# Weights of a two-layer MoE kernel converted in pairs of slots: one change to an attention and MoE kernel on Trainium2

## The chip, the core and the metric

The kernel runs on one core of one Trainium2 chip. The metric is the device time of one execution in microseconds (us). Of the engines of the core, PE does the matrix products (PEld is its weight load), DVE the vector arithmetic, ACT the activations and copies, POOL a few elementwise products, and SP issues all DMA transfers in one queue.

## The reference, cut to what matters

```python
B, H, S, D = 4, 8, 576, 64
# causal attention, mixed with a linear memory
a = softmax(causal(q @ k.T / sqrt(D)));  local = a @ v
q_p = elu(q) + 1
mem_out = (q_p @ M_prev) / (q_p @ z_prev + 1e-6)
x = sigmoid(beta) * mem_out + (1 - sigmoid(beta)) * local       # [2304, 512]
# first MLP, d_ff 1536
x = (sigmoid(x @ w_gate) * (x @ w_val)) @ w_out
# second MLP, d_ff 2048
h = x @ w_in
out = (h * clip(h + 3, 0, 6) / 6) @ w_out2
```

Everything is 32-bit. The host passes the bits of each weight array as 64-bit integers (`wm1`, `wm2`), that is, as float64 values; the kernel makes from each value a pair of 32-bit parts, a rounded high part and the rest, and every product of the MLPs is made of three matmuls (`mm3`: high by high, high by low, low by high).

## The kernel before, in words

A weight **slot** is a block of 128 by 512 weights. There are 36 slots of the first MLP (for each of the 12 blocks f of its inner width: gate, value and output) and 32 of the second. A slot takes a DMA of 512 KB into a staging tile `wst` (`w_load`, L112 to L120) and nine operations over 512 columns (`w_convert`, L122 to L144): ACT takes the absolute value of the upper words into a scratch tile `wf` (L132); DVE clamps it, masks and shifts it, joins it with the sign bits (L133 to L135: the value now stands in `wf`) and writes its power of two over the upper words (L137); ACT writes the high part of the slot from `wf` (L140); DVE scales the lower words (L141), adds them to `wf` (L142) and writes the rest to the slot (L143). The upper and lower words of a value lie side by side in `wst`, so an operation on one of them reads or writes every second word.

The kernel has three phases. **Phase A** runs attention over 80 steps (32 visits of a pair of heads and a range of tokens, three or two blocks of queries each), and between its pieces the first half of the first MLP (f 0 to 5, 18 slots) over six chunks of 312 tokens. The order of PE's instructions is written out by hand (`FILL` says how many pieces of the MLP go into a step); the order on the other engines and on SP's queue is drawn up beforehand by a list scheduler that takes what is ready, earlier program text first, and stays fixed at run time. The 18 slots are converted in steps 6 to 31, one slot in two steps of three, with two staging tiles and two scratch tiles. A chunk's input comes from attention through HBM (`xd`): `pv` drains it to `xd`, row k of `xd` being pair k of heads, and `moe_x` loads a chunk with one DMA of 624 KB into `xc` and splits it in four quarters into `xs` (ACT the high part, DVE the rest).

**Phase B** does the other half of the first MLP (f 6 to 11) over five chunks; the first of them has all 12 blocks, as its tokens were not in phase A. Its 18 new slots, and then the 32 of the second MLP, are converted as the chunks go on, with three staging and three scratch tiles (the pool `wstage2`). Its staging opens when the attention buffers are given up. **Phase C** does the second MLP over six chunks of 384 tokens.

Of the kernel before, what the change touches and what calls it, by code (L numbers as in the profile page):

```python
# [10 lines left out]
I32 = mybir.dt.int32  # L11
# [29 lines left out]
    [_T[0][0:4], _T[0][4:8], _T[0][8:12]],  # L41
    [_T[1][4 * n : 4 * n + 4] for n in range(5)],
]
NW_A = 3 * NFA
NW_B = 3 * (FF1 - NFA)
NSTAGE = 3

FILL = (4, 9, 6, 9, 6, 6)

# [14 lines left out]
class Kernel:  # L64
# [41 lines left out]
        nc.vector.tensor_scalar_add(self.a2, self.a2, 1.0)  # L106


    def plan_weights(self, keys, pools):
        self.wkeys, self.wpools, self.wstaged = list(keys), list(pools), []  # L110

    def w_load(self):  # L112
        if not self.wkeys or len(self.wstaged) >= NSTAGE:
            return
        nc = self.nc
        key = self.wkeys.pop(0)
        src = self.wm1[key[1], key[2]] if key[0] == 1 else self.wm2[key[1], key[2]]
        st = self.stage.tile([128, 512, 2], I32, name="wst", tag="wst")
        nc.sync.dma_start(st.rearrange("p a b -> p (a b)"), src.bitcast(I32))
        self.wstaged.append((key, st, self.wpools.pop(0)))  # L120

    def w_convert(self):  # L122
        if not self.wstaged:
            return
        nc = self.nc
        key, st, pool = self.wstaged.pop(0)
        lo, hi = st[:, :, 0], st[:, :, 1]


        w = self.stage.tile([128, 512], F32, name="wf", tag="wf")  # L130
        wi = w.bitcast(I32)
        nc.scalar.activation(w, hi.bitcast(F32), AF.Abs)  # L132
        nc.vector.tensor_scalar(w, w, HI_MIN, HI_MAX, op0=ALU.max, op1=ALU.min)  # L133
        nc.vector.tensor_scalar(wi, wi, 0x07FFFFFF, 3, op0=ALU.bitwise_and, op1=ALU.logical_shift_left)
        nc.vector.scalar_tensor_tensor(wi, hi, -0x40000000, wi, op0=ALU.bitwise_and, op1=ALU.bitwise_or)  # L135

        nc.vector.tensor_scalar(hi, wi, -0x800000, None, op0=ALU.bitwise_and)  # L137
        sl = pool.tile([128, 2, 512], F32R, name="wslot", tag="wslot")
        lof, hif = lo.bitcast(F32), hi.bitcast(F32)
        nc.scalar.copy(sl[:, 0, :], w)  # L140
        nc.vector.scalar_tensor_tensor(lof, lo.bitcast(U32), 2.0**-52, hif, op0=ALU.mult, op1=ALU.mult)  # L141
        nc.vector.tensor_tensor(w, w, lof, op=ALU.add)  # L142
        nc.vector.tensor_tensor(sl[:, 1, :], w, sl[:, 0, :].bitcast(F32), op=ALU.subtract)  # L143
        self.w[key] = sl  # L144

    def weight(self, *key):
        while key not in self.w:
# [24 lines left out]
    def load_visit(self, v):  # L172
        if v >= len(VISITS):
            return
        nc = self.nc
        p, ranges = VISITS[v]
        b, h = PAIRS[p]
        qk = self.pa2.tile([128, 2, S], F32, name="qk", tag="qk")
        a = self.pa2.tile([128, 20 * D], F32, name="aux", tag="aux", bufs=3)
        qn = a[:, 0 : 10 * D].rearrange("p (e j d) -> p e j d", e=2, j=5)  # L180
        (t0, n), j0, j1 = RTOK[ranges[0]], RANGES[ranges[0]][0], RANGES[ranges[0]][-1] + 1
        src = self.aux[b, h // 2]
        nc.sync.dma_start(qk[:, 0, t0 : t0 + n], self.qk[b, h // 2, :, 0, t0 : t0 + n])
        nc.sync.dma_start(qk[:, 1, : t0 + n], self.qk[b, h // 2, :, 1, : t0 + n])
        if h == 0 and 0 in ranges:
            z = self.pa2.tile([128, H, D], F32, name="zz", tag="zz")
            nc.sync.dma_start(z, self.zz[b : b + 1].rearrange("o h d -> o (h d)").broadcast_to([128, H * D]))
            self.z = z
        nc.sync.dma_start(
            qn[:, :, j0:j1, :],  # L190
            src[:, 0 : 10 * D].rearrange("p (e j d) -> p e j d", e=2, j=5)[:, :, j0:j1, :],
        )
        v1 = 10 * D + j1 * 2 * D
        nc.sync.dma_start(a[:, 10 * D : v1], src[:, 10 * D : v1])
        self.visits[v] = {
            "pair": PAIRS[p],
            "ranges": ranges,
            "z": self.z,
            "qk": qk,
            "qn": qn,  # L200
            "v": a[:, 10 * D :].rearrange("p (j c) -> p j c", j=5),
        }
# [27 lines left out]
    def score_part(self, v, i, a, e):  # L230
# [6 lines left out]
        if n == 0 and a == 0:  # L237
            P = self.pa2.tile([128, 2, 2 * PW[1]], F32, name="P", tag="P", bufs=3)
            vs["P", rg] = P[:, :, : nb * PW[rg]].rearrange("p g (n c) -> p g n c", n=nb)
            vs["l", rg] = self.pa2.tile([128, 2, nb], F32, name=f"l{rg}", tag=f"l{rg}")  # L240
            vs["m", rg] = self.pa2.tile([128, 2, nb], F32, name=f"m{rg}", tag=f"m{rg}")
# [115 lines left out]

    def moe_x(self, c):

        x = self.pm1.tile([128, KT, CA], F32, name="xc", tag="xc")  # L360
        self.nc.sync.dma_start(x, self.xd[:, :, c * CA : c * CA + CA].rearrange("k p t -> p k t"))
        xs = []
        for k in range(KT):
            t = self.pm1.tile([128, 2, CA], F32R, name=f"xs{k}", tag=f"xs{k}")
            self.split(t[:, 0], t[:, 1], x[:, k], self.nc.scalar, self.nc.vector)
            xs.append((t[:, 0], t[:, 1]))
        self.xnext = (c, xs, self.step)

# [38 lines left out]
    def phase_a(self):  # L407
        nc, tc = self.nc, self.tc
        moe_ctx, att_ctx = ExitStack(), ExitStack()
        self.stage = self.pool(att_ctx, "wstage", 2)  # L410
        self.open_moe_a(moe_ctx)
        self.open_attention(att_ctx)
        keys = [(1, f, w) for f in range(NFA) for w in range(2)] + [(1, f, 2) for f in range(NFA)]
        self.plan_weights(keys, [self.wpool] * NW_A)
        steps = [(v, rg, i) for v, (p, ranges) in enumerate(VISITS) for rg in ranges for i in RANGES[rg]]
        nt = len(steps)
# [37 lines left out]
        while t < nt or tq or vq:  # L454
# [43 lines left out]
        self.wpool2 = self.pool(ctx, "wslots2", NW_B - 4)  # L498
# [4 lines left out]
        self.wpools = [self.wpool2] * (NW_B - 4)  # L503
        for _ in range(NSTAGE):
            self.w_load()
        n = 0
        while c < NCA or stream is not None:
            self.step += 1
            moe(8)
            if n < NW_B - 4 - NSTAGE:  # L510
# [5 lines left out]
        self.wpool3 = self.pool(ctx, "wslots3", 4)  # L516
        self.wpools += [self.wpool3] * 4

        self.wpools += [self.wpool] * NW_A + [self.wpool2] * (NW_B - 4) + [self.wpool3] * 4
        self.ps_a = self.pool(ctx, "ps_a", 4, space=PSUM)  # L520

    def w_next(self):
# [19 lines left out]
    def phase_b(self):  # L542
# [49 lines left out]
        for i, item in enumerate(work):  # L592
# [10 lines left out]
    def phase_c(self):  # L603
# [40 lines left out]
        for item in work:  # L644
# [1 line left out]
            if prev:  # L646
                g4(*prev)
            prev = (gs, *item)
            for _ in range(2):
                self.w_next()  # L650
        g4(*prev)


# [58 lines left out]
```

## Time and profile before

| | |
|---|---|
| median of 3 runs | 1122.33 us (1121.84 to 1122.83) |
| the profiled execution | 1121.96 us, of which the span of its instructions is 1120.2 us |
| PE busy | 1074.1 us (96% of the span) |
| DVE busy | 616.9 us (55%) |
| ACT busy | 517.9 us (46%) |
| moved by DMA | 98.54 MB, 88 GB/s over the span |

Busy times are unions over the whole span, and the kernel has stretches with different limits; so each stretch has to be read by itself. An engine runs its instructions in order: one that waits holds up all behind it.

### The profile page before, as it was taken

How to read it: one execution, taken by the hardware profiler on the slowest of the kernel's cores; microseconds unless marked ns; L12 is line 12 of the kernel's file. 1: busy time of each engine (PE TensorE's matmuls, PEld its weight loads, DVE VectorE, ACT ScalarE, POOL GpSimd, SP SyncE). 2: the span in 40 equal slices, each digit the busy share in tenths (PEclk: the TensorE clock that was granted, in tenths of full speed). 3: DMA queues.
4: the chain of work that ended last, by engine and by line, in shares of the span. 5: the costliest groups of instructions: out<-in, count | busy, mean ns of one | idle time of the engine just before them, and what ended most of it. 6: DMA issues, size and time to landing. Idle time of an engine off the chain costs nothing.

```text
span 1120.2 us, 16105 instructions
## 1 busy us (share of the span) xinstructions
PE 1074.1 (96%) x5984; PEld 925.4 (83%) x5984; DVE 616.9 (55%) x1589; ACT 517.9 (46%) x1179; POOL 55.8 (5%) x72
## 2 busy tenths in 40 slices
PE   6679789999999999999999999999999999999998
PEld 4347567887888789999888888989999998999997
DVE  7989945455545535999997338933223232322322
ACT  5788767456745664444443123423323232332322
POOL 2102101110111000000000000000000000000000
PEclk9989889999999999999999999999999999999999
DMA  5455533233233314433653315400001010010000
GB/s 181 155 186 156 148 91 103 86 96 105 81 91 91 104 45 162 143 117 134 207 165 107 104 35 183 149 1 29 29 1 57 1 57 1 1 57 1 29 1 29
DMA packets 57935, 98.54 MB, mean 88 GB/s; under 512 B 5376, under 2 KB 42240, under 8 KB 57856
## 3 DMA queue, kind: packets, MB, share of 16 engines
q1 hardware_dynamic: 57856, 97.51, 27.4%
q8 instruction: 47, 0.77, 0.3%
q14 instruction: 32, 0.26, 0.1%
HBM read 79.50 MB, written 17.99 MB: 87 GB/s over the span
## 4 chain that ended last, share of the span: by engine, by line
PE 84%; DVE 6%; ACT 5%; DMA 4%; issue 1%; SPq 0%; POOL 0%; ACTq 0%; DVEq 0%
PE g L161 11%; PE g L159 11%; PE g L160 11%; PE acc L634 6%; PE acc L635 6%; PE acc L636 6%; PE m L159 5%; PE m L161 4%; PE m L160 4%; PE pv L338 4%; PE s L249 4%; PE t L312 3%; PE acc L159 3%; PE acc L161 3%; PE acc L160 3%; DMA wst<-in_wm 2%
## 5 line engine op out<-in xcount | busy, mean ns | idle before, releaser
L160 PE MATMUL g<-xs,wslot 128*128 128x384 f32 (+2 forms) x672 | 235.3, 351 | 0.0
L161 PE MATMUL g<-xs,wslot 128*128 128x384 f32 (+2 forms) x672 | 235.0, 351 | 0.0
L159 PE MATMUL g<-xs,wslot 128*128 128x384 f32 (+2 forms) x672 | 231.0, 351 | 0.0
L623 DVE SCALAR_TENSOR_TENSOR th<-th,g 128x384 f32<-128x384 f32 x96 | 53.1, 554 | 223.0 <-ACT th L622 222.8
L622 ACT ACTIVATE th<-g,three 128x384 f32<-128x384 f32 x96 | 55.7, 582 | 220.9 <-PE g L161 216.6
L160 PEld LDWEIGHTS g<-xs,wslot 128*128 128x128 f32 x672 | 126.1, 188 | 9.1
L159 PEld LDWEIGHTS g<-xs,wslot 128*128 128x128 f32 x672 | 126.0, 188 | 8.6
L161 PEld LDWEIGHTS g<-xs,wslot 128*128 128x128 f32 x672 | 126.1, 188 | 6.9
L634 PE MATMUL acc<-wslot,hs 128*128 128x512 f32 x288 | 113.7, 395 | 0.0
L635 PE MATMUL acc<-wslot,hs 128*128 128x512 f32 x288 | 113.5, 394 | 0.0
L270 ACT ACTIVATE P<-P,m 128x64 f32<-128x64 f32 (+4 forms) x160 | 89.3, 560 | 45.1 <-DVE m L253 42.8
L636 PE MATMUL acc<-wslot,hs 128*128 128x512 f32 x288 | 109.1, 393 | 0.0
L155 DVE TENSOR_TENSOR hs<-th,hs 128x384 fp32r<-128x384 f32 (+2 forms) x132 | 76.0, 576 | 51.6 <-ACT hs L154 51.0
L154 ACT CAST hs<-th 128x384 fp32r<-128x384 f32 (+2 forms) x132 | 69.7, 529 | 74.6 <-DVE th L623 49.5
L159 PE MATMUL m<-xs,wslot 128*128 128x312 f32 x288 | 94.3, 327 | 0.0
L312 PEld LDWEIGHTS t<-ident,P 128*128 128x128 f32 x480 | 57.5, 148 | 38.5 <-issue 20.2
L312 PE MATMUL t<-ident,P 128*128 128x128 f32 x480 | 74.4, 293 | 14.7 <-issue 5.7
L160 PE MATMUL m<-xs,wslot 128*128 128x312 f32 x288 | 88.3, 306 | 0.0
L161 PE MATMUL m<-xs,wslot 128*128 128x312 f32 x288 | 87.9, 305 | 0.0
L249 PE MATMUL s<-qk 64*128 64x320 f32 (+4 forms) x384 | 78.6, 473 | 9.6 <-DMA qk<-in_qk 6.6
L253 DVE CUSTOM_DVE_ANT_0 P<-s,mask 128x320 f32<-128x320 f32 (+3 forms) x160 | 66.1, 428 | 29.0 <-PE s L249 28.7
L132 ACT ACTIVATE wf<-wst 128x512 f32<-128x512 f32 x68 | 46.0, 677 | 77.0 <-DMA wst<-in_wm 61.5
(74 smaller groups left out, 1793.6 us busy)
## 6 DMA issues: line engine op xcount, KB each, us to landing
wst<-in_wm SPq DMA_DIRECT2D x68, 512.0 KB, 3.6
aux<-in_aux SPq DMA_DIRECT2D x32, 192.0 KB, 2.5
qk<-in_qk SPq DMA_DIRECT2D x32, 160.0 KB, 3.2
aux<-in_aux SPq DMA_DIRECT2D x16, 320.0 KB, 3.5
qk<-in_qk SPq DMA_DIRECT2D x16, 288.0 KB, 3.1
x<-x SPq DMA_DIRECT2D x6, 768.0 KB, 4.4
out<-xp SPq DMA_DIRECT2D x18, 256.0 KB, 2.0
xc<-xd SPq DMA_DIRECT2D x6, 624.0 KB, 5.0
```

Source lines behind the costliest of these rows:

```text
L154: (ehi.copy if ehi is self.nc.scalar else ehi.tensor_copy)(hi, src)
L155: elo.tensor_tensor(lo, src, hi.bitcast(F32), op=ALU.subtract)
L159: nc.tensor.matmul(out, w[0], x[0], start=first, stop=False)
L160: nc.tensor.matmul(out, w[0], x[1], start=False, stop=False)
L161: nc.tensor.matmul(out, w[1], x[0], start=False, stop=last)
L249: nc.tensor.matmul(ps[:, : e - a], qk[rows, 0, q0 : q0 + 128], qk[rows, 1, a:e], start=True, stop=True)
L253: nc.vector.tensor_tensor_reduce(out=P[:, g, n, 64 + a : 64 + e], in0=ps[:, : e - a], in1=self.mask[:, off + a : off + e], scale=-0.125, s ...
L270: self.nc.scalar.activation(x, x, AF.Exp, bias=vs["m", rg][:, g, n : n + 1], scale=-1.0, accum_out=vs["l", rg][:, g, n : n + 1],)
L312: nc.tensor.transpose(ps[:, c : c + 128], src, self.ident)
L634: nc.tensor.matmul(a, gs[:, 0, cc], w[:, 0, :], start=(f == 0), stop=False)
L635: nc.tensor.matmul(a, gs[:, 0, cc], w[:, 1, :], start=False, stop=False)
L636: nc.tensor.matmul(a, gs[:, 1, cc], w[:, 0, :], start=False, stop=(f == FF2 - 1))
```

## The change

Weights are planned, loaded, staged and released two slots at a time. In phase A one conversion covers both slots, so each of the nine operations runs over 1024 columns (`wide` 2), with one scratch tile for conversions (before: two); the value is joined in place in the staging tile and the power of two stands in the scratch tile. In phases B and C a pair is loaded together and converted one slot after the other over 512 columns (`wide` 1), with two staging tiles of two slots (before: three of one) and one scratch tile (before: three). Phase A converts a pair in every third step. A chunk's input is loaded in four DMAs of a quarter each, into two buffers. The tile for `z_prev` has one buffer instead of two, and the tiles `l` and `m` share their buffers between the two ranges.

```diff
-NW_A = 3 * NFA
-NW_B = 3 * (FF1 - NFA)
-NSTAGE = 3
+NW_A = 3 * NFA // 2
+NW_B = 3 * (FF1 - NFA) // 2
+NLATE = 2
...
     def w_load(self):
-        if not self.wkeys or len(self.wstaged) >= NSTAGE:
+        if not self.wkeys or len(self.wstaged) >= 2:
             return
...
-        st = self.stage.tile([128, 512, 2], I32, name="wst", tag="wst")
-        nc.sync.dma_start(st.rearrange("p a b -> p (a b)"), src.bitcast(I32))
+        keys = self.wkeys.pop(0)
+        n = len(keys)
+        st = self.stage.tile([128, n, 512, 2], I32, name="wst", tag="wst")
+        for i, key in enumerate(keys):
+            src = self.wm1[key[1], key[2]] if key[0] == 1 else self.wm2[key[1], key[2]]
+            nc.sync.dma_start(st[:, i].rearrange("p a b -> p (a b)"), src.bitcast(I32))
...
+    def convert(self, sl, st):
+        nc = self.nc
+        lo, hi = st[:, :, :, 0], st[:, :, :, 1]
+        w = self.stage.tile([128, self.wide, 512], F32, name="wf", tag="wf", bufs=1)
+        wi, hif, lof = w.bitcast(I32), hi.bitcast(F32), lo.bitcast(F32)
+        nc.scalar.activation(w, hif, AF.Abs)
+        nc.vector.tensor_scalar(w, w, HI_MIN, HI_MAX, op0=ALU.max, op1=ALU.min)
+        nc.vector.tensor_scalar(wi, wi, 0x07FFFFFF, 3, op0=ALU.bitwise_and, op1=ALU.logical_shift_left)
+        nc.vector.scalar_tensor_tensor(hi, hi, -0x40000000, wi, op0=ALU.bitwise_and, op1=ALU.bitwise_or)
+        nc.vector.tensor_scalar(wi, hi, -0x800000, None, op0=ALU.bitwise_and)
+        nc.scalar.copy(sl[:, 0], hif)
+        nc.vector.scalar_tensor_tensor(lof, lo.bitcast(U32), 2.0**-52, w, op0=ALU.mult, op1=ALU.mult)
+        nc.vector.tensor_tensor(hif, hif, lof, op=ALU.add)
+        nc.vector.tensor_tensor(sl[:, 1], hif, sl[:, 0].bitcast(F32), op=ALU.subtract)
 
     def w_convert(self):
...
+        keys, st, pool = self.wstaged.pop(0)
+        sl = pool.tile([128, 2, len(keys), 512], F32R, name="wslot", tag="wslot")
+        for i in range(0, len(keys), self.wide):
+            self.convert(sl[:, :, i : i + self.wide], st[:, i : i + self.wide])
+        for i, key in enumerate(keys):
+            self.w[key] = sl[:, :, i]
...
-            z = self.pa2.tile([128, H, D], F32, name="zz", tag="zz")
+            z = self.pa2.tile([128, H, D], F32, name="zz", tag="zz", bufs=1)
...
-        x = self.pm1.tile([128, KT, CA], F32, name="xc", tag="xc")
-        self.nc.sync.dma_start(x, self.xd[:, :, c * CA : c * CA + CA].rearrange("k p t -> p k t"))
         xs = []
         for k in range(KT):
+            x = self.pm2.tile([128, CA], F32, name="xc", tag="xc")
+            self.nc.sync.dma_start(x, self.xd[k, :, c * CA : c * CA + CA])
             t = self.pm1.tile([128, 2, CA], F32R, name=f"xs{k}", tag=f"xs{k}")
-            self.split(t[:, 0], t[:, 1], x[:, k], self.nc.scalar, self.nc.vector)
+            self.split(t[:, 0], t[:, 1], x, self.nc.scalar, self.nc.vector)
...
-        self.stage = self.pool(att_ctx, "wstage", 2)
+        self.stage, self.wide = self.pool(att_ctx, "wstage", 2), 2
...
-        keys = [(1, f, w) for f in range(NFA) for w in range(2)] + [(1, f, 2) for f in range(NFA)]
+        keys = [[(1, f, w) for w in range(2)] for f in range(NFA)]
+        keys += [[(1, f, 2), (1, f + 1, 2)] for f in range(0, NFA, 2)]
...
-            if t >= 6 and t % 3 < 2:
+            if t >= 6 and t % 3 == 0:
                 self.w_convert()
...
-        self.stage = self.pool(ctx, "wstage2", NSTAGE)
+        self.stage, self.wide = self.pool(ctx, "wstage2", 2), 1
...
-        keys = [(1, f, w) for f in range(NFA, FF1) for w in range(3)]
-        keys += [(2, f, w) for f in range(FF2) for w in range(2)]
+        keys = []
+        for f in range(NFA, FF1, 2):
+            keys += [[(1, f, 0), (1, f, 1)], [(1, f + 1, 0), (1, f + 1, 1)], [(1, f, 2), (1, f + 1, 2)]]
+        keys += [[(2, f, 0), (2, f, 1)] for f in range(FF2)]
...
-            for _ in range(3 if i < 12 else 1 if i < 30 else 2):
+            for _ in range(2 - i % 2 if i < 12 else i % 2 if i < 30 else 1):
                 self.w_next()
```

## Rows read from the trace of the kernel before

**Rows 1.** Stretches: length, busy us (count) of PE PEld DVE ACT POOL; PEclk; DMA; GB/s

```profile
0.00:20.00 20.00, 11.81 (x42) 7.29 (x42) 12.07 (x54) 11.30 (x36) 4.31 (x11) 1.00 0.63 203
20.00:80.00 60.00, 41.87 (x226) 25.71 (x227) 53.56 (x168) 49.18 (x125) 9.28 (x11) 0.91 0.48 158
80.00:120.00 40.00, 38.23 (x278) 30.58 (x277) 38.96 (x116) 33.83 (x96) 9.68 (x9) 1.00 0.57 170
120.00:142.00 22.00, 13.94 (x67) 9.39 (x65) 21.11 (x57) 15.48 (x44) 2.94 (x4) 0.72 0.43 127
142.00:200.00 58.00, 54.09 (x344) 40.21 (x345) 26.19 (x102) 37.91 (x94) 5.87 (x8) 0.93 0.33 94
200.00:430.00 230.00, 228.82 (x1622) 190.67 (x1621) 112.28 (x421) 133.13 (x352) 23.77 (x30) 1.00 0.29 86
430.00:600.00 170.00, 169.57 (x863) 157.38 (x863) 158.21 (x316) 76.21 (x139) 0.00 (x0) 1.00 0.51 166
600.00:1110.00 510.00, 510.00 (x2528) 459.78 (x2527) 193.43 (x361) 158.21 (x293) 0.00 (x0) 1.00 0.13 41
```

**Rows 2.** What PE waited for, 0 to 150 us: total us, times, longest

```profile
PE m L161 <- DVE wslot L143: 6.8, 4, 3.6
PE t L312 <- issue: 5.7, 2, 5.4
PE m L159 <- ACT wslot L140: 1.1, 1, 1.1
```

**Rows 3.** DVE's groups over the span by shape: busy us, mean ns | idle before

```profile
L141 DVE SCALAR_TENSOR_TENSOR wst<-wst 128x512 f32<-128x512 uint32 x68 | 46.5, 684 | 0.1
L143 DVE TENSOR_TENSOR wslot<-wf,wslot 128x512 fp32r<-128x512 f32 x68 | 46.4, 682 | 0.0
L137 DVE TENSOR_SCALAR wst<-wf 128x512 int32<-128x512 int32 x68 | 30.2, 445 | 0.1
...
L133 DVE TENSOR_SCALAR wf<-wf 128x512 f32<-128x512 f32 x68 | 28.5, 420 | 13.3 <-ACT wf L132 12.9
...
L155 DVE TENSOR_TENSOR xs<-xc,xs 128x312 fp32r<-128x312 f32 x24 | 11.3, 495 | 14.6 <-ACT xs L154 14.6
```

**Rows 4.** DVE in order of time, two places: start us, us, instruction

```profile
100.12 0.67 DVE L143 TENSOR_TENSOR wslot<-wf,wslot 128x512 fp32r<-128x512 f32 x1
100.72 0.42 DVE L137 TENSOR_SCALAR wst<-wf 128x512 int32<-128x512 int32 x1
101.05 0.46 DVE L387 SCALAR_TENSOR_TENSOR th<-th,m 128x312 f32<-128x312 f32 x1
...
138.57 0.42 DVE L134 TENSOR_SCALAR wf<-wf 128x512 int32<-128x512 int32 x1
139.03 0.69 DVE L135 SCALAR_TENSOR_TENSOR wf<-wst,wf 128x512 int32<-128x512 int32 x1
...
141.01 0.69 DVE L142 TENSOR_TENSOR wf<-wf,wst 128x512 f32<-128x512 f32 x1
141.74 0.69 DVE L143 TENSOR_TENSOR wslot<-wf,wslot 128x512 fp32r<-128x512 f32 x1
```

**Rows 5.** ACT's two conversion groups over the span, by shape

```profile
L132 ACT ACTIVATE wf<-wst 128x512 f32<-128x512 f32 x68 | 46.0, 677 | 77.0 <-DMA wst<-in_wm 61.5 <-DVE wslot L143 5.0 <-DVE wf L142 3.3
...
L140 ACT CAST wslot<-wf 128x512 fp32r<-128x512 f32 x68 | 42.0, 617 | 33.3 <-DVE wf L135 27.0 <-PE g L161 6.0
```

**Rows 6.** What ACT waited for, 0 to 143 us

```profile
ACT wf L132 <- DMA wst<-in_wm: 8.8, 9, 2.0
```

**Rows 7.** ACT in order of time around the first chunk's input

```profile
65.57 1.51 ACT L154 CAST xs<-xc 128x312 fp32r<-128x312 f32 x4 [2.00 <-DMA xc<-xd]
```

**Rows 8.** Phase B: the first absolute value on ACT, in order of time

```profile
433.58 0.66 ACT L132 ACTIVATE wf<-wst 128x512 f32<-128x512 f32 x1 [0.63 <-DMA wst<-in_wm]
```

**Rows 9.** Phase B: slots finished by DVE from 430 to 510.7 us

```profile
L143 DVE TENSOR_TENSOR wslot<-wf,wslot 128x512 fp32r<-128x512 f32 x17 | 11.6, 683 | 0.0
```

**Rows 10.** Phase B: PE in order of time, output products of block f 10

```profile
525.34 0.75 PE L159 MATMUL acc<-hs,wslot 128*128 128x432 f32 x3
```

More of the change, by code (lines that the diff above doesn't have):

```diff
@@ L106, in attn_consts, with plan_weights @@
         nc.vector.tensor_scalar_add(self.a2, self.a2, 1.0)
-    def plan_weights(self, keys, pools):
-        self.wkeys, self.wpools, self.wstaged = list(keys), list(pools), []
+    def plan_weights(self, groups, pools):
+        self.wkeys, self.wpools, self.wstaged = list(groups), list(pools), []
     def w_load(self):
-        if not self.wkeys or len(self.wstaged) >= NSTAGE:
+        if not self.wkeys or len(self.wstaged) >= 2:
             return
         nc = self.nc
-        key = self.wkeys.pop(0)
-        src = self.wm1[key[1], key[2]] if key[0] == 1 else self.wm2[key[1], key[2]]
-        st = self.stage.tile([128, 512, 2], I32, name="wst", tag="wst")
-        nc.sync.dma_start(st.rearrange("p a b -> p (a b)"), src.bitcast(I32))
-        self.wstaged.append((key, st, self.wpools.pop(0)))
+        keys = self.wkeys.pop(0)
[4 more added lines that the diff above has]
+            nc.sync.dma_start(st[:, i].rearrange("p a b -> p (a b)"), src.bitcast(I32))
+        self.wstaged.append((keys, st, self.wpools.pop(0)))
+    def convert(self, sl, st):
[12 more added lines that the diff above has]
+        nc.vector.tensor_tensor(sl[:, 1], hif, sl[:, 0].bitcast(F32), op=ALU.subtract)
     def w_convert(self):
@@ L125, in w_convert @@
         nc = self.nc
[L126 to L144, printed above, removed]
+        keys, st, pool = self.wstaged.pop(0)
[4 more added lines that the diff above has]
+            self.w[key] = sl[:, :, i]
     def weight(self, *key):
@@ L239, in score_part @@
             vs["P", rg] = P[:, :, : nb * PW[rg]].rearrange("p g (n c) -> p g n c", n=nb)
-            vs["l", rg] = self.pa2.tile([128, 2, nb], F32, name=f"l{rg}", tag=f"l{rg}")
-            vs["m", rg] = self.pa2.tile([128, 2, nb], F32, name=f"m{rg}", tag=f"m{rg}")
+            vs["l", rg] = self.pa2.tile([128, 2, 3], F32, name="l", tag="l")[:, :, :nb]
+            vs["m", rg] = self.pa2.tile([128, 2, 3], F32, name="m", tag="m")[:, :, :nb]
         P, m, qk = vs["P", rg], vs["m", rg], vs["qk"]
@@ L495, in phase_a @@
         ctx = self.ctx
-        self.stage = self.pool(ctx, "wstage2", NSTAGE)
+        self.stage, self.wide = self.pool(ctx, "wstage2", 2), 1
         self.bx = self.pool(ctx, "bx", 1)
-        self.wpool2 = self.pool(ctx, "wslots2", NW_B - 4)
+        self.wpool2 = self.pool(ctx, "wslots2", NW_B - NLATE)
         self.ps_g = self.pool(ctx, "ps_g", 4, space=PSUM)
-        keys = [(1, f, w) for f in range(NFA, FF1) for w in range(3)]
-        keys += [(2, f, w) for f in range(FF2) for w in range(2)]
+        keys = []
+        for f in range(NFA, FF1, 2):
+            keys += [[(1, f, 0), (1, f, 1)], [(1, f + 1, 0), (1, f + 1, 1)], [(1, f, 2), (1, f + 1, 2)]]
+        keys += [[(2, f, 0), (2, f, 1)] for f in range(FF2)]
         self.plan_weights(keys, [])
-        self.wpools = [self.wpool2] * (NW_B - 4)
-        for _ in range(NSTAGE):
+        self.wpools = [self.wpool2] * (NW_B - NLATE)
+        for _ in range(2):
             self.w_load()
@@ L509, in phase_a @@
             moe(8)
-            if n < NW_B - 4 - NSTAGE:
+            if n < NW_B - NLATE - 2:
                 self.w_next()
@@ L515, in phase_a @@
         self.br = self.pool(ctx, "br", 1, side="right")
-        self.wpool3 = self.pool(ctx, "wslots3", 4)
-        self.wpools += [self.wpool3] * 4
-        self.wpools += [self.wpool] * NW_A + [self.wpool2] * (NW_B - 4) + [self.wpool3] * 4
+        self.wpool3 = self.pool(ctx, "wslots3", NLATE)
+        self.wpools += [self.wpool3] * NLATE
+        self.wpools += [self.wpool] * NW_A + [self.wpool2] * (NW_B - NLATE) + [self.wpool3] * NLATE
         self.ps_a = self.pool(ctx, "ps_a", 4, space=PSUM)
@@ L648, in phase_c @@
             prev = (gs, *item)
-            for _ in range(2):
-                self.w_next()
+            self.w_next()
         g4(*prev)
```

## The prediction

> **What bounds the kernel now.** I read the busy times by stretch first, since the page's averages mix stretches with different limits. From 200 us to 1110 us PE is busy for 908.4 of 910 us [rows 1]: the matmuls are the limit there, and DVE and ACT count only if they make PE wait. Before 200 us PE is idle 40 us: 8.2 us in the first 20 (first transfers), 18.1 from 20 to 80, 1.8 from 80 to 120, 8.1 from 120 to 142, and 3.9 after [rows 1]. From 20 to 142 us DVE is busy 113.6 of 122 us [rows 1]; it is the fullest engine there, with attention and the 18 conversions of phase A. So the change can be paid only out of the 28 us that PE idles between 20 and 142, or by making PE wait later.
>
> Then I asked what ended PE's waits in the first 150 us. Some 7.9 us end at the two operations that finish a slot, L143 and L140 [rows 2]: PE stands at output matmuls of the first chunk until its last weights are there. The last slot's L143 runs at 141.74 us [rows 4], just where the idle stretch ends. One wait of 5.4 us [rows 2] falls at 62 us, when ACT stands 2.0 us before the first chunk's input has landed [rows 7] and the rescaling of P, which PE's transposes want, is queued behind it. So the place where this change acts is the pace at which 18 slots get through DVE up to 142 us.
>
> **The change part by part.**
>
> *Fewer, longer operations in phase A.* Nine pairs replace 18 slots, so 9 x 7 = 63 DVE instructions vanish: 36 of the wide form (about 0.68 us for 512 columns) and 27 of the form that takes 0.42 us [rows 3]. Only the fixed part is saved. For the wide form, 512 columns take 0.682 us and 312 take 0.495 [rows 3], 0.94 ns a column, so 512 more columns cost 0.48 us; I take half of that, 0.24, for the fast form, which at 0.42 us cannot be going at that rate. How much of the fixed part is seen depends on the neighbour. With unrelated neighbours an operation follows a wide one after 0.60 us and a fast one after 0.33 us [rows 4]; fixed parts 0.12 and 0.09, so 36 x 0.12 + 27 x 0.09 = 6.8 us. Where each needs the one before, the starts are 0.73 and 0.46 us apart [rows 4]; fixed parts 0.25 and 0.22, or 14.9 us. The first is nearer: the stretch has two conversions and attention mixed. Against it: one scratch tile allows only one conversion in flight, so more of the operations left have their own predecessor as neighbour, at 0.13 us each (0.73 less 0.60), 63 x 0.13 = 8.2 us if all were mixed before and none after. I charge a third, 2.7. Net gain 4.0 us; bounds -1.4 to +14.9.
>
> *Strides.* The value now stands in every second word. L141 already reads and writes such words and takes 0.684 us against 0.682 for L143, with two dense operands [rows 3], so the wide form pays nothing. L137 writes them at 0.445 against 0.420 for L133 [rows 3]; reading them in the fast form isn't shown, and if it fell to the wide rate, nine masks would cost 9 x 2 x 0.26 = 4.7 us. I take 0, since the write does not fall. ACT's copy L140 becomes a strided read like L132: 0.677 against 0.617 [rows 5], 18 x 0.06 = 1.1 us more, against fixed parts of 18 ACT instructions saved. I take 0 for ACT; it has 23.5 us free from 20 to 142 [rows 1].
>
> *Deeper staging in phase A.* Two tiles of two slots hold twice as much ahead. ACT waits 8.8 us for staged weights in the first 143 us [rows 6], and DVE has 8.4 us of idle time from 20 to 142 [rows 1]. A wait ends later on both sides: the tile is now held to the last subtraction, and a pair's load is two DMAs. I take +2.0 us, a quarter; bounds 0 and 8.4. The price at the start: two more slots, 1 MB, go before the next visits' loads; at the 203 GB/s of the first stretch [rows 1] that is 5.2 us if all of it is in the way. The second `z_prev` buffer, 256 KB, may then no longer be loaded there, and DVE has converted slots to work on. I charge 1.0; bounds 0 and 5.2.
>
> *The input in quarters.* Row k of `xd` comes from one pair of heads, so three quarters needn't wait for the last pair. The third and fourth wait, in SP's queue, for ACT and DVE to free a buffer, and the loads of weights, queries and values behind them wait too. For the first chunk, ACT's 2.0 us [rows 7] and part of PE's 5.4 us [rows 2] can go; a late third quarter can cost the same again. I take +0.5; bounds -2 and +5.4. Later chunks have cover: PE idles 1.2 us from 200 to 430 us [rows 1].
>
> *Pairs as units.* The first slot of a pair is ready only when the second is. In the tail up to 142 us PE waits for the last one anyway, and from 80 to 120 us it is 96% busy [rows 1], so the first chunk's earlier weights had cover. I take 0.
>
> *Phases B and C.* Columns per operation stay, so DVE's work stays. What goes is the overlap: the next absolute value, on ACT, cannot start before the previous scaling L141 has read the one scratch tile. It has the addition and the subtraction behind it as cover, 2 x 0.73 = 1.46 us for 0.66 us [rows 4, 8]. Before, 17 slots took 77.1 us from the first absolute value at 433.58 us [rows 8, 9], 4.54 each; mixed, a slot's own operations take 4 x 0.60 + 3 x 0.33 = 3.39 [rows 4], which leaves 1.15 for the rest. One conversion at a time takes 4 x 0.73 + 3 x 0.46 = 4.30, so 4.30 to 5.45 with the rest. PE wants the 17th slot for block 10 at 525.34 us [rows 10]: allowed 91.8 / 17 = 5.40 each. I take 4.9 and no wait: 0, down to -1. Phase C's weights are converted where DVE has room: 38% busy from 600 us on [rows 1]. A fourth staged slot ahead of phase B's first input is 512 KB, 3 us at the 166 GB/s of that stretch [rows 1]; the tail of phase A's chunks on PE covers it.
>
> *Sum.* 4.0 + 2.0 - 1.0 + 0.5 = 5.5 us. The profiled execution took 1121.96 us (span 1120.2, 1.8 around it), 0.4 under the median of the three runs: 1116.5 us.
>
> **The rivals.** I call 0.2%, 2.2 us, about what a measurement here can tell from no change.
>
> *The whole fixed part comes back.* If the 63 instructions were worth their dependent spacing, 14.9 us, less the startup's 1.0 and with half of the staging wait, 4, the gain is 18; with only two thirds of it on PE's path, 12: 1110 us, reach 1106 to 1113. For it: the tail that PE waits on ends in dependent operations [rows 4], and ACT's waits for staging are real. Against it: PE's idle time from 80 to 120 us is only 1.8 us, so much of the gain there buys nothing. The Trainium skill ("VectorE: DVE Perf Modes", "The DRAIN you can't avoid") has a next operation start only when the pipe is empty, which would make the whole fixed part count; by its figure of 151 cycles at 0.96 GHz, 63 instructions are an estimated 9.9 us. This trace does not agree for mixed work: L137 starts at 100.72 us, 0.07 us before the L143 in front has ended [rows 4]. Chance 0.21.
>
> *The change gives its gain back.* One conversion in flight takes the whole 8.2 us, or the 1 MB at the start takes 5.2: 1120 to 1124 us, about 1122. For it: DVE has only 7% of idle time to lose [rows 1]. Chance 0.17.
>
> *Slower: phase B runs short of weights.* If ACT's absolute value is queued late (behind a tanh that waits for PE), its 0.66 us is not covered and a slot takes 5.45 + 0.66 = 6.1 us: the 17th is ready at 433.6 + 104 = 537.6, PE waits 12.3 us, less 5.5 gained, 1129 us. It decides from 433.6 + 17p > 525.3 + 5.5 + 2.2, p = 5.85 us a slot. For it: DVE is 93% busy there [rows 1]. Against: today's pace leaves 14.6 us in hand. Chance 0.14.
>
> **How the numbers follow.** The forecast, a gain of 2.2 to 8.5 us (1113.5 to 1119.8), has 0.48. Faster by over 0.2% are it and the first rival, 0.69; within 0.2% the second, 0.17; slower the third, 0.14. From 1108 to 1124.5 us lie the forecast, the second rival and some four fifths of the first, 0.82; the bounds of the unknown costs (startup -5.2, staging up to 8.4) end inside it.
>
> **What would show it.** Right: seven DVE groups of nine over 1024 columns in phase A at about 1.16 us (wide) and 0.66 us (fast); the last slot done some 5 us before 141.7 us and PE's waits on L143's successor cut by half; PE still 100% busy from 430 us. Wrong: a mask operation near 1.16 us (strided reads fall to the slow rate); PE idle in the first 20 us above 8.2 us by the startup's loads; PE waits on a scratch or slot tile between 490 and 540 us; SP held by the input's quarters before 200 us.

## The result, and the profile after

The changed kernel takes 1106.3 us (median of 4 runs, 1105.09 to 1108.91) against 1122.58 us for the kernel before in the same job: 16.3 us less. The ratio of the comparison is 0.987 [0.9853, 0.9888], which is 14.6 us (12.6 to 16.5); where kernels of different jobs are compared below, ratios are used. The forecast was 1116.5 us with a range of 1108 to 1124.5; the time lies below it. The direction was right, and the gain forecast, 5.5 us, was about a third of what came. One execution of a later kernel (the addition on POOL) took 1674.18 us at a granted clock of 0.577 and is left out below.

The profiled execution took 1105.09 us, of which the span is 1103.3 us, 16.9 us less than before. The head of the profile's page of the changed kernel:

```profile
span 1103.3 us, 16108 instructions
...
PE 1068.7 (97%) x5984; PEld 921.0 (83%) x5984; DVE 625.0 (57%) x1526; ACT 521.9 (47%) x1161; POOL 58.5 (5%) x72
```

Its stretches of busy time, with the columns of [rows 1]:

```profile
0.00:20.00 20.00, 12.64 (x50) 8.02 (x51) 12.79 (x52) 11.50 (x35) 5.72 (x12) 1.00 0.68 243
20.00:80.00 60.00, 43.90 (x241) 27.30 (x241) 59.23 (x157) 52.88 (x124) 12.42 (x12) 0.86 0.55 175
80.00:120.00 40.00, 39.10 (x287) 31.15 (x282) 38.51 (x95) 36.13 (x96) 7.46 (x9) 1.00 0.51 165
120.00:142.00 22.00, 19.64 (x121) 14.48 (x120) 20.27 (x57) 16.64 (x50) 3.71 (x5) 1.00 0.67 220
142.00:200.00 58.00, 56.18 (x393) 44.08 (x392) 33.85 (x124) 41.02 (x104) 7.35 (x9) 0.97 0.29 88
200.00:430.00 230.00, 228.48 (x1592) 190.53 (x1591) 118.44 (x416) 132.80 (x341) 21.89 (x28) 1.00 0.32 99
430.00:600.00 170.00, 170.00 (x844) 156.39 (x843) 151.47 (x281) 74.04 (x128) 0.00 (x0) 1.00 0.40 136
```

Against [rows 1] the 16.9 us divide in two. PE's idle time before 200 us falls from 40.1 to 28.5 us, 11.5 less: 0.8 in the first 20, 2.0 from 20 to 80, 0.9 from 80 to 120, 5.7 from 120 to 142, and 2.1 after. The other 5.4 us are busy time: the same 5984 matmuls keep PE busy 1068.7 us instead of 1074.1. The granted clock goes with it: 0.72 from 120 to 142 us before, 1.00 now; 0.93 and 0.97 from 142 to 200; against that 0.91 and 0.86 from 20 to 80. From 200 us on PE is all but full in both.

One number takes in both parts: the matmuls recorded before 200 us, the counts of the first five stretches. Before, 42 + 226 + 278 + 67 + 344 = 957; now 50 + 241 + 287 + 121 + 393 = 1092. At 228.48 / 1592 = 0.144 us for one in the stretch behind, 135 more by 200 us are 19.4 us of work that is not left for later. It overstates the 16.9 a little (the mix of shapes differs), but it goes with the time in all kernels below, and the table at the end of the experiments uses it. It is bookkeeping, not a cause: the matmuls are the same in number, so those not done by 200 us come later.

What PE and ACT waited for up to 143 us, and two of SP's waits, after two of SP's waits in the kernel before:

```profile
SPq L119 <- DVE wf L142: 28.8, 8, 10.4
SPq L361 <- DMA xd<-xpr: 2.3, 1, 2.3
```

```profile
PE m L171 <- DVE wslot L143: 1.9, 1, 1.9
...
ACT wf L134 <- DMA wst<-in_wm: 0.3, 1, 0.3
...
SPq L124 <- DVE wslot L143: 17.7, 4, 9.3
SPq L373 <- DMA xd<-xpr: 13.2, 7, 2.5
```

PE's waits on a slot fall from 7.9 us [rows 2] to 1.9, and ACT's waits for staged weights from 8.8 us [rows 6] to 0.3. The largest of SP's own waits for a staging tile was 28.8 us in eight waits in the kernel before; it is 17.7 in four. In exchange SP stands 13.2 us at the quarters of the input, which wait for attention's rows (2.3 us before).

DVE's groups of the pairs, by shape, and the one-slot form of the mask for comparison; then DVE in order of time at the last slot and at the first conversion of phase B:

```profile
L137 DVE SCALAR_TENSOR_TENSOR wst<-wst,wf 128x1024 int32<-128x1024 int32 x9 | 11.0, 1217 | 0.0
L143 DVE TENSOR_TENSOR wslot<-wst,wslot 128x1024 fp32r<-128x1024 f32 x9 | 10.9, 1216 | 0.1
...
L139 DVE TENSOR_SCALAR wf<-wst 128x1024 int32<-128x1024 int32 x9 | 7.6, 849 | 0.0
...
L139 DVE TENSOR_SCALAR wf<-wst 128x512 int32<-128x512 int32 x50 | 21.3, 425 | 1.1
...
126.96 1.22 DVE L143 TENSOR_TENSOR wslot<-wst,wslot 128x1024 fp32r<-128x1024 f32 x1
...
133.25 0.43 DVE L135 TENSOR_SCALAR wf<-wf 128x512 f32<-128x512 f32 x1 [0.73 <-ACT wf L134]
```

The last slot ends at 128.2 us instead of 142.4 [rows 4]: 14.2 us earlier, where the prediction said some 5. DVE's idle time from 20 to 80 us is gone (59.23 of 60 busy). The Trainium skill ("VectorE: DVE Perf Modes", the section on the TRN2 errata) puts the overhead of an operation on SBUF at a fixed amount per instruction; these rows agree: 1024 columns take 1.216 us, two operations of 512 take 2 x 0.682 [rows 3], so 0.15 us is saved for each operation taken away. "Vector Engine (DVE) Microarchitecture Reference" of the Trainium skill (section 5.2) gives 1.0417 ns a column; here (1216 - 682) / 512 is 1.043.

### The profile page after: what moved, and what is told of

It reads as the page before. It is cut to its first block, busy times and chain, and to the rows that moved or that the text cites. A ratio compares the mean times of both kernels' runs of the same rounds, so it can differ in the third digit from the quotient of the medians.

```text
span 1103.3 us, 16108 instructions
## 1 busy us (share of the span) xinstructions
PE 1068.7 (97%) x5984; PEld 921.0 (83%) x5984; DVE 625.0 (57%) x1526; ACT 521.9 (47%) x1161; POOL 58.5 (5%) x72
## 4 chain that ended last, share of the span: by engine, by line
PE 84%; DVE 6%; DMA 4%; ACT 3%; issue 1%; SPq 0%; POOL 0%; ACTq 0%; DVEq 0%
PE g L171 12%; PE g L170 12%; PE g L169 11%; PE acc L647 6%; PE acc L648 6%; PE acc L649 6%; PE m L169 5%; PE m L171 4%; PE m L170 4%; PE pv L348 4%; PE t L322 3%; PE s L259 3%; PE acc L171 3%; PE acc L169 3%; PE acc L170 3%; DMA xc<-xd 2%
## 5 line engine op out<-in xcount | busy, mean ns | idle before, releaser
L325 ACT COPY T<-t 128x512 f32<-128x512 f32 (+2 forms) x128 | 66.1, 541 | 9.8 <-PE t L322 9.7
```

The costliest lines, as they stand in the source:

```text
L325: nc.scalar.copy(pr["T", rg][:, o : o + c], ps[:, :c])
```

## The experiments

Each time below is a median beside the median of the kernel before in the same job; ratios carry their 95% interval. The changed kernel stands at 0.987.

**One slot at a time, still one scratch tile** (the changed kernel, phase A converting 512 columns per operation):

```diff
-        self.stage, self.wide = self.pool(att_ctx, "wstage", 2), 2
+        self.stage, self.wide = self.pool(att_ctx, "wstage", 2), 1
```

> The changed kernel, but in phase A a pair is converted slot by slot over 512 columns (one scratch tile); loads in pairs, staging and quarters stay. Theory columns (the gain comes from 63 fewer DVE operations): the last slot of phase A is done at 136 us or later instead of 128.3, PE waits on it for 4 us or more, and the time goes back to 1114 to 1120 us. Theory staging (the gain comes from loads that are ahead, ACT's 8.8 us of waits): the last slot stays before 131 us and the time at 1105 to 1110 us.

Measured: 1134.37 us against 1120.84, ratio 1.0115 [1.0094, 1.0135]. Both theories miss the time: it is some 27 us over the changed kernel and slower than the kernel before, though the marks of theory columns (a last slot after 136 us, PE waiting on slots for over 4 us) are there. A stretch of its busy times, and PE's largest waits on slots up to 200 us:

```profile
120.00:142.00 22.00, 9.21 (x25) 5.42 (x25) 20.75 (x47) 9.88 (x22) 0.70 (x1) 0.61 0.24 81
...
PE m L171 <- DVE wslot L143: 12.0, 7, 3.1
...
PE m L169 <- ACT wslot L140: 6.3, 5, 2.0
```

PE is busy 9 of 22 us there, and up to 200 us it stands 18.3 us at slots; the last one ends at 144.1 us. Two explanations remain: DVE's throughput with twice as many instructions, or the latency of one conversion after another through a single scratch tile.

**The same with two scratch tiles** separates them:

```diff
-        w = self.stage.tile([128, self.wide, 512], F32, name="wf", tag="wf", bufs=1)
+        w = self.stage.tile([128, self.wide, 512], F32, name="wf", tag="wf", bufs=self.nwf)
...
-        self.stage, self.wide = self.pool(att_ctx, "wstage", 2), 2
+        self.stage, self.wide = self.pool(att_ctx, "wstage", 2), 1
+        self.nwf = 2
...
+        self.nwf = 1
```

> The changed kernel with conversions over 512 columns in phase A, as in e1_narrow, but with two scratch tiles there, so that two conversions can be under way. Theory latency (what sets the pace of slots is the time from one absolute value to the scaling that frees the scratch tile; 1024 columns halve the number of such chains, two scratch tiles overlap them): the last slot moves back from 148 to 134 to 139 us and the time to 1110 to 1117 us, near e3_deep. Theory throughput (the sum of DVE's durations sets it, which e1_narrow and this kernel share): 1128 to 1137 us.

Measured: 1111.86 us against 1121.58, 0.9913 [0.9899, 0.9928]. So it was latency (the last slot ends at 131.3 us, earlier still than that theory had it; it was 144.1 with one tile, not 148): the second scratch tile is worth 1.0115 - 0.9913 of 1122 us, 22.7 us, at the same number of instructions. Seen from this kernel, the step to 1024 columns with one scratch tile is worth 0.9913 - 0.987, 4.8 us; from the kernel with one scratch tile it is worth 27.

**Quarters from the other side** (the kernel before, its input loaded in quarters, the tile for `z_prev` single, `l` and `m` shared between ranges; the staging and the conversions stay):

```diff
-        x = self.pm1.tile([128, KT, CA], F32, name="xc", tag="xc")
-        self.nc.sync.dma_start(x, self.xd[:, :, c * CA : c * CA + CA].rearrange("k p t -> p k t"))
...
+            x = self.pm2.tile([128, CA], F32, name="xc", tag="xc")
+            self.nc.sync.dma_start(x, self.xd[k, :, c * CA : c * CA + CA])
```

> The kernel before, with only the input in quarters, one buffer for z_prev and the shared l and m tiles. Theories columns and staging both: within 2 us of the kernel before (1120 to 1124 us). Theory quarters (ACT no longer stands before the first chunk's input, so the 5.4 us wait of PE goes): 1115 to 1119 us.

Measured: 1127.5 us against 1120.84, 1.0057 [1.0038, 1.0076]: 6.4 us slower, which no theory had. To see whether the tiles or the quarters do it, the quarters were put in alone:

> The kernel before with the four quarter loads of a chunk's input alone; the tiles for z_prev, l and m as before. Theory quarters cost (the third and fourth quarter wait in SP's queue and hold up loads behind them): 1125 to 1129 us, as e2_quarters. Theory tiles cost (one buffer for z_prev or the shared l and m tiles make e2_quarters slower): 1119 to 1122 us.

Measured: 1126.09 us against 1121.58, 1.0040 [1.0028, 1.0053]: 4.5 us slower by the quarters alone. Its waits of ACT and of SP up to 143 us, and its stretch from 160 to 200 us:

```profile
ACT wf L132 <- DMA wst<-in_wm: 9.8, 6, 3.3
...
SPq L363 <- DMA xd<-xpr: 15.6, 6, 4.0
...
160.00:200.00 40.00, 34.05 (x226) 25.62 (x227) 17.36 (x68) 27.59 (x67) 3.86 (x6) 0.96 0.33 98
```

SP, which issues everything in one queue, is held 15.6 us by quarters that wait for attention's rows to reach HBM; the kernel before shows 2.3 us of this. PE does 226 matmuls from 160 to 200 us; the kernel before does 251 there.

**Depth alone** (the kernel with quarters, and four staging tiles of one slot in phase A; 512 columns and two scratch tiles stay):

```diff
+        self.nst = 4
...
-        st = self.stage.tile([128, 512, 2], I32, name="wst", tag="wst")
+        st = self.stage.tile([128, 512, 2], I32, name="wst", tag="wst", bufs=self.nst)
...
-            if len(self.wstaged) < 2:
+            for _ in range(2):
                 self.w_load()
```

> The kernel before with the quarters and four staging tiles of one slot in phase A (as many slots ahead as in the changed kernel), conversions over 512 columns with two scratch tiles as before. Theory staging: ACT's waits for staged weights fall below 2 us, the last slot of phase A is done by 132 us, 1106 to 1113 us. Theory columns: DVE has the same work, the last slot stays after 136 us, 1116 to 1122 us.

Measured: 1113.72 us against 1120.84, 0.9932 [0.9912, 0.9952]. Against the kernel with quarters in the same job that is 13.8 us for depth (by the ratios 14.0, uncertain by some 3), in a kernel with the quarters; against the kernel before, depth, quarters and tiles together gain 7.1 us. Two of its stretches, and ACT's wait for staged weights up to 143 us:

```profile
20.00:80.00 60.00, 46.42 (x242) 28.83 (x242) 57.20 (x179) 51.97 (x132) 10.87 (x12) 0.86 0.54 171
...
142.00:200.00 58.00, 55.86 (x381) 43.11 (x378) 35.41 (x127) 41.41 (x101) 5.99 (x8) 0.97 0.40 114
...
ACT wf L132 <- DMA wst<-in_wm: 1.2, 1, 1.2
```

ACT's waits fall as theory staging had it, and the time is just past its range; its other mark, a last slot by 132 us, did not come. The last slot ends at 137.0 us, only 1.9 us before that of the kernel with quarters. Most of the gain lies behind it (the two profiled executions differ by 8.9 us): 381 matmuls from 142 to 200 us, where the kernel with quarters has 332 and the kernel before 344 [rows 1].

**Half the depth** (the changed kernel with one staging tile of two slots in phase A):

```diff
-        self.stage, self.wide = self.pool(att_ctx, "wstage", 2), 2
+        self.stage, self.wide = self.pool(att_ctx, "wstage", 1), 2
```

> The changed kernel with one staging tile of two slots in phase A instead of two, so that a pair is loaded only when the pair before is done. Theory staging (depth is worth about half of the gain or more): each of seven loads adds 4 to 5 us to the time between pairs, the last slot ends after 150 us, 1125 to 1150 us. Theory columns alone: below 1112 us.

Measured: 1154.05 us against 1121.58, 1.0285 [1.0268, 1.0302], some 47 us over the changed kernel and beyond even the range of theory staging. The last slot's subtraction starts at 169.44 us:

```profile
142.00:200.00 58.00, 33.60 (x170) 22.85 (x170) 26.06 (x65) 23.48 (x52) 2.68 (x4) 0.70 0.31 96
...
169.44 1.23 DVE L143 TENSOR_TENSOR wslot<-wst,wslot 128x1024 fp32r<-128x1024 f32 x1
```

DVE is busy less than half of this stretch, so it isn't DVE's sum that holds the slots back; with one tile a load cannot begin before the conversion in front has ended.

**The clock** (the kernel before with 33 matmuls added, whose product nobody reads, in places where PE waits for the last slots):

```diff
+    nc.tensor.matmul(out, w[0], x[1], start=False, stop=False)
+    fill = self.ps_v.tile([128, 512], F32, name="fill", tag="pv")
+    n = self.left.pop(0)
+    for j in range(n):
+        nc.tensor.matmul(fill[:, :CA], self.w[1, 0, 0][:, 0, 0:128], x[0], start=(j == 0), stop=(j == n - 1))
+    nc.tensor.matmul(out, w[1], x[0], start=False, stop=last)
```

> The kernel before, with 33 extra matmuls (312 columns, results thrown away) put into the places of the first chunk's output products where PE waits for its last weights: 9, 18 and 6, some 1.3, 2.6 and 0.9 us of work. Theory clock (part of the gain is PE's granted clock, 0.72 from 120 to 142 us before and 1.00 after, because PE idles less): the granted clock from 120 to 160 us is 0.95 or more and the kernel gets faster by 2 to 6 us although it does more. Rival (PE's idle time alone counts): no faster, up to 5 us slower.

Measured: 1121.26 us against 1120.84 with a ratio of 0.9998 [0.9982, 1.0014]: no change. Its stretches, its line of busy times, and PE in order of time at the largest block of added matmuls:

```profile
120.00:142.00 22.00, 15.95 (x102) 12.71 (x101) 21.04 (x58) 15.18 (x45) 3.62 (x4) 0.97 0.44 138
...
142.00:160.00 18.00, 18.00 (x101) 13.40 (x100) 7.12 (x27) 10.31 (x26) 1.34 (x2) 0.84 0.26 77
160.00:200.00 40.00, 35.59 (x251) 27.56 (x249) 19.68 (x77) 28.52 (x72) 4.53 (x6) 1.00 0.35 102
...
PE 1076.6 (96%) x6017; PEld 930.2 (83%) x6017; DVE 615.9 (55%) x1589; ACT 517.8 (46%) x1179; POOL 55.7 (5%) x72
...
130.97 2.75 PE L706 MATMUL fill<-ha,wslot 128*128 128x312 f32 x18
...
135.01 0.41 PE L707 MATMUL m<-ha,wslot 128*128 128x312 f32 x1 [1.29 <-DVE wslot L143]
```

The granted clock from 120 to 142 us rises to 0.97 (0.72 before [rows 1]), that is from a mixture with the 1.2 GHz level to nearly all 2.4 GHz, and the matmul behind the block still waits 1.29 us for its slot. From 142 to 160 us it stays low, 0.84, so theory clock's condition (0.95 up to 160 us) was not met in full. The slots were as late as ever: the last one ends at 143.5 us. The time can't price the clock by itself: the 33 added matmuls are some 4.8 us of work at 0.144 us each, and PE is busy 1076.6 us here against 1074.1 before, so by this estimate the clock gave back some 2.3 us and the added work took more. What is shown is that filling PE's waits, with the clock that comes of it, gains nothing while the slots stay late.

**DVE's room** (the changed kernel, the addition of a pair's parts moved from DVE to POOL):

```diff
-        nc.vector.tensor_tensor(hif, hif, lof, op=ALU.add)
+        (nc.gpsimd if self.wide == 2 else nc.vector).tensor_tensor(hif, hif, lof, op=ALU.add)
```

> The changed kernel with the addition of phase A's conversions (nine, 1024 columns, 1.31 us each on DVE) moved to POOL, which is idle for 90% of that stretch. Theory DVE-bound (from 20 to 128 us DVE's work is the limit): the last slot ends at 118 to 125 us and the time falls to 1098 to 1104 us. Rival (POOL's addition, some 3 us by its products of 384 columns at 1.1 us, lengthens each conversion and holds its staging tile): 1106 us or more.

Measured: 1109.36 us (three runs) against 1121.58, 0.9887 [0.9871, 0.9904], not faster than 0.987, as the rival had it. The profile is of the same kernel in another job:

> A profile of e8_pool. If POOL's addition lengthens each conversion, the additions take over 2 us each and the last slot ends no earlier than the 128.2 us of the changed kernel; if DVE gained, the last slot ends before 125 us and the time was lost elsewhere.

It took 1109.8 us in its one run, the kernel before 1121.38. Its additions, DVE's subtractions by shape from 20 to 130 us, and POOL and DVE in order of time at the last slot:

```profile
L142 POOL TENSOR_TENSOR wst<-wst 128x1024 f32<-128x1024 f32 x9 | 17.3, 1924 | 25.5 <-DVE nr L237 6.5 <-DVE l L303 5.8 <-DVE wst L141 3.5
...
L143 DVE TENSOR_TENSOR wslot<-wst,wslot 128x1024 fp32r<-128x1024 f32 x9 | 12.7, 1414 | 0.0
...
122.69 1.22 POOL L295 TENSOR_TENSOR P<-ph,nr 128x384 f32<-128x384 f32 x1
123.87 1.25 POOL L233 TENSOR_TENSOR phw<-ph,zz 128x384 f32<-128x384 f32 x1
...
124.17 2.03 DVE L143 TENSOR_TENSOR wslot<-wst,wslot 128x1024 fp32r<-128x1024 f32 x1
```

Neither reading of the expectation came out whole: the additions take just under 2 us, and the last slot ends at 126.2 us, 2.0 us before the changed kernel's. DVE is busy 6.0 us less from 20 to 142 us, but PE has done no more work by 200 us than in the changed kernel (table below). An addition takes POOL 1.92 us against 1.31 on DVE, and a subtraction that begins while POOL is at work grows to 2.03 us, the mean from 1.22 to 1.41. So DVE's sum alone is no longer what sets PE's pace here.

**The quarters in the changed kernel.** A whole load needs room, so two output buffers of attention and of the chunks are single in all three of these; the control has that alone:

```diff
-        x = self.pa2.tile([128, 320], F32, name="xpr", tag="xpr")
+        x = self.pa2.tile([128, 320], F32, name="xpr", tag="xpr", bufs=1)
...
-            o = self.pm2.tile([128, CA], F32, name="xp", tag="xp")
+            o = self.pm2.tile([128, CA], F32, name="xp", tag="xp", bufs=1)
```

> The changed kernel with one buffer instead of two for the drain tiles xpr and xp and nothing else, the control for e9_whole and e10_quarters4: 1105 to 1109 us, as the changed kernel, since each of these tiles is drained by a DMA long before the next is written.

Measured: 1109.62 us against 1121.38, 0.9891 [0.9876, 0.9906]; 0.2% over the changed kernel and just past what was expected. With the whole chunk in one DMA again:

```diff
+        xa = self.pm1.tile([128, KT, CA], F32, name="xc", tag="xc")
+        self.nc.sync.dma_start(xa, self.xd[:, :, c * CA : c * CA + CA].rearrange("k p t -> p k t"))
...
-            x = self.pm2.tile([128, CA], F32, name="xc", tag="xc")
-            self.nc.sync.dma_start(x, self.xd[k, :, c * CA : c * CA + CA])
+            x = xa[:, k]
```

> The changed kernel with a chunk's input loaded whole again, by one DMA into a tile of four quarters; to make room for it, the drain tiles xpr and xp have one buffer instead of two. Theory quarters cost (they cost 4.5 us in the kernel before, and cost the same here): 1100 to 1104 us, a version faster than both. Rival (the quarters cost time only while the weights' loads, too, stand in SP's queue for lack of staging): within 2 us of e11_control.

Measured: 1115.4 us, 0.9933 [0.9915, 0.9951]: 5.8 us slower than the control (4.7 by the ratios). Theory and rival both miss. With the quarters in four buffers instead of two (`bufs=4` at `xc`):

> The changed kernel with four buffers for the quarters of a chunk's input, so that none waits for a split to free one; drain tiles as in e9_whole. If the quarters cost time by waiting for a buffer: as e9_whole, 1100 to 1104 us. If by being issued early and waiting for attention's write in SP's queue: as e11_control.

Measured: 1108.78 us, 0.9886 [0.9871, 0.9901], the control's time; waiting for a free buffer costs nothing. The busy lines of the pages of the whole load and of the control, in that order, and SP's wait in the former:

```profile
PE 1077.9 (97%) x5984; PEld 926.9 (83%) x5984; DVE 623.6 (56%) x1526; ACT 521.6 (47%) x1161; POOL 58.9 (5%) x72
```

```profile
PE 1071.0 (97%) x5984; PEld 923.2 (83%) x5984; DVE 624.2 (56%) x1526; ACT 523.2 (47%) x1161; POOL 58.6 (5%) x72
```

```profile
SPq L371 <- DMA xd<-xpr: 7.6, 1, 7.6
```

With the whole load SP is held once, for 7.6 us. The loss is not in PE's idle time, which is 30.0 us before 200 us in both, but in its busy time: 6.9 us more for the same matmuls. The granted clock is 0.80 from 20 to 80 us with the whole load (0.86 in the control), and from 142 to 160 us it is 0.81 (0.95 in the control):

```profile
20.00:80.00 60.00, 45.01 (x218) 26.22 (x215) 57.40 (x147) 48.70 (x113) 10.39 (x11) 0.80 0.52 164
...
142.00:160.00 18.00, 15.10 (x74) 10.20 (x74) 10.20 (x34) 10.47 (x24) 2.04 (x3) 0.81 0.33 92
```

So the same edit costs 4.5 us in the surroundings of the kernel before and is worth 5.8 us in those of the kernel after.

**All kernels side by side.** Matmuls recorded before 200 us (sums of the counts of the five stretches) against the profiled execution of each:

| kernel | matmuls before 200 us | last slot ends, us | profiled execution, us |
|---|---|---|---|
| after, one staging tile | 756 | 170.7 | 1155.23 |
| after, 512 columns, one scratch | 863 | 144.1 | 1134.89 |
| before, quarters alone | 934 | 142.1 | 1126.24 |
| before | 957 | 142.4 | 1121.96 |
| before, quarters and tiles | 961 | 139.0 | 1123.67 |
| before, added matmuls (33 of 994, not counted) | 961 | 143.5 | 1124.20 |
| after, whole load | 1015 | 125.5 | 1115.90 |
| before, quarters, tiles, four staging tiles | 1017 | 137.0 | 1114.74 |
| after, 512 columns, two scratch | 1044 | 131.3 | 1111.90 |
| after, addition on POOL | 1057 | 126.2 | 1109.80 |
| after, four buffers for the quarters | 1059 | 130.9 | 1108.52 |
| after, control of the whole load | 1063 | 130.7 | 1110.04 |
| after | 1092 | 128.2 | 1105.09 |

From 756 to 1092 the time falls by 50.1 us, 0.149 us a matmul, near the 0.144 that one takes where PE is full; no kernel leaves the straight line between the ends by more than 4.4 us. The end of the last slot orders them less well: the whole load has the earliest last slot and is 10.8 us behind the changed kernel.

## Why the prediction was too small

**The step that failed: "Deeper staging in phase A", +2.0 us, bounds 0 and 8.4, added to the quarters as if the two were independent.** Beside the quarters, depth measured 13.8 us, beyond the bound. The mechanism was named rightly: ACT's 8.8 us of waits for staged weights [rows 6] are 0.3 us now. The term was mis-sized, and the fault is in the bound: 8.4 us was DVE's idle time from 20 to 142 us, so the gain was measured on the engine that converts, and up to the end of the last slot. What counts is PE. Slots that come earlier let PE's other matmuls move up, also after the last slot: with depth that slot came 1.9 us earlier and PE did 49 matmuls more from 142 to 200 us than with the quarters in the staging of before. And the conversion chain, load to slot, has a latency that no sum of DVE's busy times shows: with one staging tile it cost 47 us while DVE stood idle for more than half of the stretch from 142 to 200 us.

The 13.8 us are not what depth is worth everywhere. The quarters alone cost 4.5 us; quarters, tiles and depth together gain 7.1 us, where the prediction's terms (+2.0, -1.0 for the startup, +0.5) add to 1.5. The changed kernel with the whole load, and the control's single drain tiles, gains 7.5 us in all (0.9933). Depth with the whole load in the kernel before was not run, so how much of the gain is depth's own and how much comes of depth and quarters together stays open.

**"the change can be paid only out of the 28 us that PE idles between 20 and 142".** That held for 8.6 of the 11.5 us of idle time that went, but 5.4 us came out of PE's busy time, which the sentence left out. The row was there: a granted clock of 0.72 from 120 to 142 us [rows 1], in the stretch with PE's waits. The added matmuls show that raising it while the slots stay late gains nothing; what the clock alone is worth no run shows. The whole load points to its having a price: as much idle time as the control, and 6.9 us more of busy time at a lower clock.

**Columns, +4.0 us.** Two scratch tiles and 512 columns against one and 1024 differ by 4.8 us (from 0.0043, whose two intervals leave about 2.6 us either way): about right as a net. The two halves of it were not. The charge of 2.7 us for one conversion in flight was worked out for pairs of slots; at 512 columns one scratch tile costs 22.7 us. The pair is what makes one scratch tile bearable: half as many trips through the chain. Pairs with two scratch tiles were not run, so the gain of wider operations and the price of the single tile are known only as this net. The first rival, "The whole fixed part comes back", named 1106 to 1113 us, and the time is at its edge, but its reason was 14.9 us from the columns, and they gave 4.8. Its figure was near for the wrong cause.

**Quarters, +0.5 us, bounds -2 and +5.4.** Both bounds were passed: -4.5 us in the kernel before, +5.8 in the kernel after. What was foreseen, that SP's queue is held, is seen in both (15.6 and 13.2 us). Why the sign turns is not settled. It may be that a held queue costs less when weights are staged deeper, but that is argued, not shown, and the loss of the whole load shows as busy time at a lower clock, not as idle time.

**What held.** Strides, 0: the mask of 512 strided words takes 0.425 us against 0.420 for a fast operation on dense words [rows 3], and 1024 take 0.68 to 0.70 in seven of nine, far from the wide form's 1.22; the mean of 0.849 comes from two of 1.41 and 1.43 beside POOL's products (last section). Phases B and C, 0: PE is busy 170.00 of 170 us from 430 us (169.57 before). ACT, 0: it has 16.4 us left from 20 to 142 (23.5 before [rows 1]), and PE's wait of 1.1 us for its copy of a slot [rows 2] is gone. Pairs as units, 0: no run took this apart; PE waits on a slot once, for 1.9 us. The startup's charge of 1.0 us did not appear: PE's idle time in the first 20 us is 7.4 us (8.2 before), while the DMA moves 243 GB/s (203 before).

By ratios, from the kernel before to the kernel after: quarters and tiles +6.4 us (1.0057), depth -14.0 (to 0.9932), and all the rest -7.0 (to 0.987). The rest is what is left over, wider operations, one scratch tile and the pairs' order together; only its part that the columns give (4.8 us) has a comparison of its own. Each of these steps is uncertain by some 2 to 3 us, and holds in this order only.

## What to carry to other kernels

A deeper staging buffer is priced at the engine that waits for the result, over the whole stretch in which its work can move up, not by the idle time of the engine that converts; here that was 13.8 us, beside the quarters, against an assumed 2. Two changes that act on one queue, such as depth and finer loads, are not to be added as if each were worth the same without the other. Scratch tiles and operation width must be judged together: this chain of dependent operations wanted either two in flight or half as many trips (22.7 us lay between one and two scratch tiles at 512 columns, while 1024 columns did with one). Work done by the critical engine at a fixed time (here matmuls by 200 us) told these variants apart better than the end of the last conversion, or than idle time alone.

## What the runs showed of the hardware that was not expected

- The granted clock fell where PE waited at slots: 0.50 from 130 to 140 us in the kernel before, that is the 1.2 GHz level. With those waits filled it was 0.97 over 120 to 142 us (and 0.84 from 142 to 160) at an unchanged total (0.9998).

```profile
130.00:140.00 10.00, 5.52 (x18) 3.27 (x17) 9.89 (x24) 4.32 (x12) 1.64 (x2) 0.50 0.40 123
```

- A DVE operation of a conversion was stretched where it began while a POOL product was running (and more than 0.05 us of it was left), and not where the product began after it; this holds for all of the changed kernel's up to 200 us. There the mask at 119.86 us, begun 0.13 us behind a product, took 1.43 us instead of 0.68; the subtraction at 67.33 us, with a product beginning 0.15 us later and running on past its end, took 1.18 us, no longer than the others. The subtraction of 2.03 us above, 1.22 us otherwise, began 0.30 us behind a product.

```profile
119.73 1.01 POOL L233 TENSOR_TENSOR phw<-ph,zz 128x384 f32<-128x384 f32 x1 [0.49 <-DVE ph L231]
119.86 1.43 DVE L139 TENSOR_SCALAR wf<-wst 128x1024 int32<-128x1024 int32 x1
...
67.33 1.18 DVE L143 TENSOR_TENSOR wslot<-wst,wslot 128x1024 fp32r<-128x1024 f32 x1
67.48 1.51 POOL L295 TENSOR_TENSOR P<-ph,nr 128x256 f32<-128x256 f32 x1 [4.72 <-DVE l L304]
```

- Phase B's staging opened 300 us before phase B: on DVE its first conversion begins at 133.25 us and stops before the addition, which comes at 414.17 us. By their sizes its tiles (18 KB a partition) fit where phase A's staging was (20 KB; before, 18 against 12), so they need not wait for the attention buffers, as they do in the kernel before. Four other kernels bear this out: those with 18 or 20 KB there (512 columns with one scratch tile or two, and four staging tiles) begin between 137 and 149 us, the one with a single staging tile of two slots (12 KB) does not. PE is full from 200 us on, so no gain was seen from it.

```profile
414.17 0.69 DVE L142 TENSOR_TENSOR wst<-wst 128x512 f32<-128x512 f32 x1 [3.93 <-ACT wslot L140]
```
